# A Nyström attention feeding a squared-ReLU MLP: written step order for the first batch, its inverse folded into A, batch 1's inverse in 32x32 blocks, loads of batches 1 and 2 into an idle buffer

## The chip, the cores and the metric

One core of a Trainium2 chip. The time is the device time of one execution in microseconds, median of several runs. Before the change it is 268.99 us (268.72 to 269.55, three runs). Engines: PE is the matmul engine, DVE VectorE, ACT ScalarE, POOL GpSimd.

## The reference

```python
# q, k, v: (8 batches, 8 heads, 576, 64); m = 32 landmarks of 18 rows each
A  = softmax(q @ k_lm.T / 8)          # 576 x 32
Bm = softmax(q_lm @ k_lm.T / 8)       # 32 x 32
C  = softmax(q_lm @ k.T / 8)          # 32 x 576
Z  = Bm.T / (norm1(Bm) * norminf(Bm) + 1e-6)
for _ in range(6):
    Z = 2 * Z - Z @ Bm @ Z            # Newton inverse
x = (A @ Z @ C @ v)                   # all heads side by side: (4608, 512)
out = square(relu(x @ w_in)) @ w_out  # 512 -> 2048 -> 512
```

## The kernel before

The kernel never forms x. It multiplies the small C v (here cvb) with Z and the input weights to a matrix G, and computes h = G^T A^T straight from it: 16 products "h" of 128 x 576 for a batch (four matmuls of 128x288 each; the timelines count these matmuls), then relu on ACT, square on DVE, and 72 matmuls "out" of the second product. While the MLP of batch b runs, the attention of batch b+1 is prepared in the gaps. A plan of words says in which order PE, DVE and ACT get their instructions:

```python
BATCH0 = (   # h: one product of the MLP; s: its square; a number: so many outs
    "h h s s g h pk s h s h h g s h s h s tk0 h h s pq mk s h s h mq tq0 h s s 2 lm ls s h "
    "tk1 ib tq1 1 h h 1 tt 1 if 2 s 1 sq0 1 jo s 2 sq1 jo s 1 tl jo 2 as0 3 sk1 jl 3 ar0 3 "
    "sk0 2 as1 1 nu at0 2 ar1 nn pk+ 1 cv 1 nu nn1 1 at1 wt pq+ 2 gg0 2 gg1"
)
# pk/pq: cast of the next batch's k/q (with +: of the one after that); tk/tq: its transposes;
# mk/mq: landmark means; ib/if: begin of the inverse; jo: joint step (EY); jl: last joint y;
# nu, nn: Newton steps; tl: tails; as/ar/at: A's row sums, rows, transposes; wt: C's fold; gg: G
```

The words of the inverse and the loads ahead of it, cut:

```python
def products(diagonal, moving):            # eight matmuls 32x32, or two 128x128
    n, w = moving(0).shape[-1], diagonal.shape[-1]
    res = ntile([P, 2, n], place=1, placed=b >= PLACED)
    for qd in range(2):
        for a in range(0, P, w):
            nc.tensor.matmul(res[a:a + w, qd, :], lhsT=diagonal[a:a + w, qd, :], ...)

def stationary(src, tag):                  # batch 0: src itself ("compact")
    ...                                    # other batches: spread on DVE to a block diagonal
with tc.issue_after(one.ins):              # loads after the first piece of w_in
    load_v(0, loaded[0])
    for j in range(1, 4):
        w_in(j)                            # input weights, four pieces
    load_qk(1, loaded[1])
    for j in range(4): ...                 # output weights, four pieces
    load_v(1, loaded[1])
```

The head (batch 0's own attention) is a generator with 17 idle matmuls in it, `warm(n)`, which keep PE's clock up.

The softmax here doesn't subtract the row's maximum and nothing guards it: scores larger than these inputs give would overflow.

Of the kernel before, what the change touches and what calls it, by code (L numbers as in the profile page):

```python
# [17 lines left out]
B = 8  # L18
# [14 lines left out]
PLACED = 1  # L33
BATCH0 = (
    "h h s s g h pk s h s h h g s h s h s tk0 h h s pq mk s h s h mq tq0 h s s 2 lm ls s h "
    "tk1 ib tq1 1 h h 1 tt 1 if 2 s 1 sq0 1 jo s 2 sq1 jo s 1 tl jo 2 as0 3 sk1 jl 3 ar0 3 "
    "sk0 2 as1 1 nu at0 2 ar1 nn pk+ 1 cv 1 nu nn1 1 at1 wt pq+ 2 gg0 2 gg1"
)
BATCH1 = (
    "1 mk 1 h tq0 1 h mq h s tq1 2 lm h s 1 s h ls 1 tt s 1 s h ib sq0 h s 2 h tl 1 if 4 s "  # L40
    "sq1 as0 2 jo h tk0 s 1 h jo 1 s tk1 1 pk+ 1 h jo s pq+ 1 sk0 1 as1 3 sk1 1 jl ar0 s h 1 "
    "h ar1 cv 1 nu h 1 s h nn at0 3 nu 1 s 1 h nn1 3 s 1 wt at1 2 s 2 s 1 gg0 8 gg1 12"
)
EVEN = (
    "2 h h 2 s s 1 mk mq 1 h 1 s 3 lm h ls 1 sq0 h 1 s 1 h 1 s ib 3 s tl h 2 if sq1 h as1 3 "
    "jo sk0 h pk+ 2 s as0 2 s 2 jo s 1 h sk1 h 2 s h pq+ jo cv 2 jl s 1 ar0 2 h h 1 s nu 1 "
    "ar1 2 h nn s 1 s h at0 s 3 nu 3 at1 1 nn1 4 wt s 4 gg0 5 gg1 7"
)
ODD = (
    "2 h s mk 1 h 1 h mq 1 h 2 lm 1 s ls 1 s h s 4 s sq0 1 ib h 1 s tl if 2 h 1 sq1 h pk+ 1 "  # L50
    "jo s as0 s 1 h 1 sk0 2 s 1 h 1 sk1 jo 1 s 1 h as1 h jo s pq+ 1 cv jl 4 h s ar0 1 nu h "
    "ar1 3 s 1 nn h 3 s at0 h 1 nu at1 1 s 1 nn1 3 s 3 wt 4 gg0 8 gg1 15"
)
LAST = (
    "1 h h 1 s 4 h 1 s s h 1 h 2 s 1 h 1 s 6 s 1 h s h 3 h s 2 h 1 s 2 s 1 h 2 s 3 h 2 s h h "
    "1 s 3 h 4 h 7 s s s"
)
PLANS = [BATCH0, BATCH1, EVEN, ODD, EVEN, ODD, EVEN, LAST]
# [3 lines left out]
def kernel(  # L62
# [31 lines left out]
    vts, ects = [], []  # L94
# [7 lines left out]

    def load_qk(b: int, X: dict):

        X["qkt"] = loads.tile([P, H, D], BF16, tag="qkt", name="qkt")

        def tails():
            for src, r0 in ((k, TAIL), (q, 0)):
                nc.gpsimd.dma_start(X["qkt"][r0:r0 + TAIL, :, :],  # L109
                              src[b, :, NC4 * P:S, :].rearrange("h p d -> p h d"))  # L110

        if b > 0:
            tails()
        for nm, src in (("k", k), ("q", q)):
            if b == 0 and nm == "k":
                X[nm + "raw"] = mlp.tile([P, H, NC4, D], F32, tag="gT", name="raw")
            else:
                X[nm + "raw"] = loads.tile([P, H, NC4, D], BF16, tag="raw", name="raw")
            parts = ((0, H // 2), (H // 2, H)) if b == 0 and nm == "q" else ((0, H),)
            for lo, hi in parts:  # L120
                (nc.sync if b == 0 and nm == "k" else nc.gpsimd).dma_start(  # L121
                    X[nm + "raw"][:, lo:hi, :, :],
                    src[b, lo:hi, 0:NC4 * P, :].rearrange("h (p c) d -> p h c d", c=NC4)
                )
            if b == 0 and nm == "k":
                tails()

    def load_v(b: int, X: dict):
        X["vm"] = loads.tile([P, H, NC4, D], BF16, tag="vm", name="vm")
        X["vt"] = vts[b % 2]  # L130
        nc.gpsimd.dma_start(
            X["vm"][:], v[b, :, 0:NC4 * P, :].rearrange("h (p c) d -> p h c d", c=NC4)
        )
        nc.gpsimd.dma_start(
            X["vt"][P - TAIL:P, :, :], v[b, :, NC4 * P:S, :].rearrange("h p d -> p h d")
# [9 lines left out]
    seg = const.tile([P, NC4 + 2, M], BF16, name="seg")  # L145
# [16 lines left out]
    nc.vector.tensor_copy(blk_bf[:], blk[:])  # L162
    ones_bf = const.tile([P, 1], BF16, name="ones_bf")
# [5 lines left out]
    def load_rest(after):  # L169

        def w_in(j):

            r0, f0 = 256 * (j % 2), 1024 * (j // 2)
            return nc.gpsimd.dma_start(
                w_in_bf[64 * (j % 2):64 * (j % 2) + 64, :, f0:f0 + 1024],
                moe_w_in[r0:r0 + 256, f0:f0 + 1024].rearrange("(j d) f -> d j f", d=D),
            )

        with tc.issue_after(masked.ins):
            one = w_in(0)  # L180
# [4 lines left out]
        with tc.issue_after(one.ins):  # L185
            load_v(0, loaded[0])
            for j in range(1, 4):
                w_in(j)
            load_qk(1, loaded[1])
            for j in range(4):  # L190
                nc.gpsimd.dma_start(
                    w_out_bf[:, 4 * j:4 * j + 4, :],
                    moe_w_out[512 * j:512 * j + 512, :].rearrange("(ft fp) c -> fp ft c", fp=P),
                )
            load_v(1, loaded[1])
# [8 lines left out]
    def prepare(b: int, nms=("k", "q"), halves=((0, H),)):  # L204

        X = loaded[b]
        for nm in nms:
            if nm not in X:
                X[nm] = loads.tile([P, NC4, H, D], BF16, tag=nm + "nat", bufs=1, name="nat")
                X[nm + "T"] = attn.tile([P, NC4, NPAIR, P], BF16, tag=nm + "T", name="T")  # L210
            raw = X[nm + "raw"].rearrange("p h c d -> p c h d")
            if b == 0:
                for lo, hi in halves if nm == "q" else ((0, H),):
                    if nm == "q":
                        nc.vector.tensor_copy(X[nm][:, :, lo:hi, :], raw[:, :, lo:hi, :])
                        continue
                    nc.vector.tensor_copy(X[nm][:, 0:2, lo:hi, :], raw[:, 0:2, lo:hi, :])
                    X["cast"] = nc.scalar.copy(X[nm][:, 2:4, lo:hi, :], raw[:, 2:4, lo:hi, :])
                continue
            nc.vector.tensor_copy(X[nm][:], raw)  # L220
            if b >= DMA_T:
                nc.sync.dma_start_transpose(
                    X[nm + "T"].rearrange("p c a t -> p (c a) t"),
                    X[nm].rearrange("p c h d -> p (c h d)"))
        if "k" in nms:
            X["tT"] = attn.tile([P, NPAIR, P], BF16, tag="tT", name="tT")
            if b >= DMA_T:
# [9 lines left out]
    mark, begin, front = [], [], []  # L237

    def in_turn():
        return tc.issue_after(front[0].ins) if front else nullcontext()  # L240

    def attention(b: int, R: dict):
# [4 lines left out]
        first = b == 0  # L247

        def transposed(nm, half):
            if not first:  # L250
                tps = ntile([P, 2, NPAIR, P], BF16, place=int(nm == "q"), placed=b >= PLACED)[:]
            else:
                if half == 0:
                    X["tps"] = psum.tile([P, 4, NPAIR, P], BF16, tag="h", bufs=2, name="tps")
                tps = X["tps"][:, 2 * half:2 * half + 2, :, :]
# [9 lines left out]
        def transposed_tail():  # L265
            tps = ntile([P, NPAIR, P], BF16, placed=b >= PLACED)
# [4 lines left out]
            nc.vector.tensor_copy(X["tT"][:], tps[:])  # L271

        means = ntile([P, 2, NPAIR, M], placed=b >= PLACED)
        STk = small.tile([P, NPAIR, M], BF16, tag="STk", name="STk")

        def segment_means(ti, nm):
# [5 lines left out]
            with in_turn() if b == 1 else nullcontext():  # L282
                for n, (p, c) in enumerate(order):
                    src = X[nm][:, c, 2 * p:2 * p + 2, :] if c < NC4 else X["qkt"][:, 2 * p:2 * p + 2, :]
                    nc.tensor.matmul(  # L285
                        means[:, ti, p, :],
                        lhsT=src.rearrange("p h d -> p (h d)"),
# [566 lines left out]
```

## Time and profile before

| | before |
|---|---|
| span of the profiled run | 267.4 us |
| first h of batch 0 | 24.99 us |
| batch 1's k turned by PE, from | 30.60 us |
| 16th h of batch 0 ends | 38.38 us |
| batch 1's first joint product | 40.02 us |
| first h of batch 1, of batch 2 | 54.81, 84.69 us |

The times come from PE's timeline. From the first h on PE is the bound; what a stage can win is seen from when the next batch's first h starts.

### The profile page before, as it was taken

What the parts mean: (1) busy time and instruction counts of PE and PEld (TensorE: products, weight loads), DVE (VectorE), ACT (ScalarE), POOL (GpSimd) and SP (SyncE); (2) the same over time, 40 slices, a digit from 0 to 9 for tenths busy, and PEclk for the clock granted to TensorE, in tenths of its full rate; (3) what the DMA queues carried; (4) which work ended last, traced back from release to release, by engine and by line L of the source; (5) the groups of instructions that cost most, each with busy time, mean ns of one, the idle gap of its engine ahead of it and who ended that gap; (6) DMA issues with size and microseconds to landing.
All of it is one profiled execution on the core that took longest, in us unless ns stands there. A gap on an engine that the chain in (4) does not pass through costs nothing.

```text
span 267.4 us, 6750 instructions
## 1 busy us (share of the span) xinstructions
PE 247.7 (93%) x2752; PEld 151.0 (56%) x2793; DVE 177.4 (66%) x492; ACT 156.9 (59%) x278; POOL 45.5 (17%) x70
## 2 busy tenths in 40 slices
PE   2988999699989999999999999999999999999994
PEld 0754675276645665466546666466536665555443
DVE  4585989769983699559953798569943887443000
ACT  2366895377844774478345855487535955566210
POOL 8844233402400213021300122000000000000000
PEclk9997999999999999999999999999999999999999
DMA  8999999999699949995996579974421111111222
GB/s 184 177 204 196 204 205 189 206 210 165 103 161 214 126 95 158 142 206 99 201 159 132 78 94 171 168 134 110 90 81 40 42 39 42 39 43 39 78 81 78
DMA packets 69791, 34.65 MB, mean 130 GB/s; under 512 B 37376, under 2 KB 64256, under 8 KB 69760
## 3 DMA queue, kind: packets, MB, share of 16 engines
q0 software_dynamic: 39808, 17.83, 54.9%
q1 hardware_dynamic: 24704, 7.08, 17.7%
q10 hardware_dynamic: 5248, 9.31, 10.5%
q8 instruction: 22, 0.36, 0.6%
q14 instruction: 9, 0.07, 0.1%
HBM read 36.70 MB, written 9.44 MB: 173 GB/s over the span
## 4 chain that ended last, share of the span: by engine, by line
PE 60%; DVE 22%; DMA 6%; ACT 6%; issue 4%; POOL 2%; ACTq 0%; POOLq 0%; DVEq 0%
PE ops L732 18%; PE n L732 15%; PE h L700 14%; DMA raw<-in_q_dram 6%; DVE gT L708 5%; PE g L639 3%; DVE ra L464 3%; ACT r L707 3%; PE n L285 2%; DVE nat L220 2%; PE n L357 2%; PE n L486 2%; DVE ED L348 1%; DVE EY L362 1%; DVE rra L469 1%
## 5 line engine op out<-in xcount | busy, mean ns | idle before, releaser
L707 ACT ACTIVATE r<-h 128x576 bf16<-128x576 f32 x128 | 81.3, 655 | 40.6 <-PE h L700 30.1
L700 PE MATMUL h<-AT,G 128*128 128x288 bf16 x512 | 81.0, 286 | 0.7 <-ACT r L707 0.4
L732 PE MATMUL ops<-w_out_bf,gT 128*128 128x512 bf16 (+1 forms) x301 | 76.7, 368 | 1.0 <-issue 0.5
L708 DVE TENSOR_TENSOR gT<-r 128x576 bf16<-128x576 bf16 x128 | 55.5, 446 | 31.5 <-ACT r L707 30.7
L732 PEld LDWEIGHTS <-gT 128*128 128x128 bf16 x592 | 53.4, 97 | 40.6 <-issue 5.1
L732 PE MATMUL n<-w_out_bf,gT 128*128 128x512 bf16 x253 | 67.6, 379 | 0.9 <-issue 0.5
L700 PEld LDWEIGHTS <-G 128*128 128x128 bf16 x512 | 47.5, 98 | 22.3 <-issue 1.5
L628 DVE CAST G<-g 128x1024 bf16<-128x1024 f32 x14 | 17.1, 1224 | 10.5 <-PE g L639 10.5
L628 ACT CAST G<-g 128x1024 bf16<-128x1024 f32 x14 | 14.2, 1013 | 14.7 <-PE g L639 14.7
L743 ACT COPY o_sb<-ops 128x512 f32<-128x512 f32 (+1 forms) x19 | 10.9, 576 | 12.3 <-PE ops L732 11.9
L743 ACT COPY o_sb<-n 128x512 f32<-128x512 f32 x17 | 10.0, 585 | 10.9 <-PE n L732 10.3
L109 POOL DMA_DIRECT2D qkt<-in_k_dram x8 | 5.7, 708 | 54.3 <-PE n L295 42.7
L440 PEld LDWEIGHTS <-T 128*128 128x128 bf16 x256 | 11.2, 98 | 4.3 <-issue 1.0
L464 DVE TENSOR_REDUCE ra<-EA 128x20 f32<-128x640 f32 (+1 forms) x19 | 13.4, 705 | 0.3
L476 DVE TENSOR_TENSOR an<-EA,rra 128x640 bf16<-128x640 f32 (+2 forms) x17 | 13.1, 771 | 0.0
L440 PE MATMUL n<-bd,T 128*128 128x64 bf16 x256 | 12.7, 193 | 0.2
L357 PEld LDWEIGHTS <-ED 128*128 128x128 bf16 x84 | 7.1, 97 | 9.3 <-DVE ED L348 5.9
L121 POOL DMA_DIRECT2D raw<-in_k_dram x7 | 6.2, 884 | 32.4 <-DVE EY L362 12.4
L444 ACT ACTIVATE EA<-n 128x512 f32<-128x512 f32 x16 | 9.5, 595 | 2.3 <-PE n L440 2.3
L444 ACT ACTIVATE EC<-n 128x512 bf16<-128x512 f32 x16 | 9.6, 598 | 2.1 <-PE n L440 2.1
L220 DVE COPY nat<-raw 128x2048 bf16<-128x2048 bf16 x14 | 10.3, 734 | 0.6 <-DMA raw<-in_q_dram 0.4
L639 PE MATMUL g<-w_in_bf,WT 64*32 64x512 bf16 x232 | 9.6, 390 | 0.7 <-ACT G L628 0.4
(121 smaller groups left out, 268.1 us busy)
## 6 DMA issues: line engine op xcount, KB each, us to landing
out_dram<-o_sb ACTq DMA_DIRECT2D x31, 256.0 KB, 3.2
vm<-in_v_dram POOLq DMA_DIRECT2D x8, 512.0 KB, 16.4
raw<-in_k_dram POOLq DMA_DIRECT2D x7, 512.0 KB, 9.9
raw<-in_q_dram POOLq DMA_DIRECT2D x7, 512.0 KB, 13.8
w_in_bf<-in_moe_w_in_dram POOLq DMA_DIRECT2D x4, 512.0 KB, 10.7
w_out_bf<-in_moe_w_out_dram POOLq DMA_DIRECT2D x4, 512.0 KB, 16.1
out_dram<-o_sb ACTq DMA_DIRECT2D x9, 128.0 KB, 3.2
raw<-in_k_dram SPq DMA_DIRECT2D x1, 1024.0 KB, 5.3
```

The lines of the kernel that those rows point to most:

```text
L220: nc.vector.tensor_copy(X[nm][:], raw)
L440: nc.tensor.matmul(sc[:, c, j, :, :], lhsT=X[nm + "T"][:, c, p, :], rhs=BD[:, 1 if nm == "q" else 0, p, 0:64], start=True, stop=True)
L444: nc.scalar.activation((EA if nm == "q" else EC)[:, qd, 0:NC4, :], sc.rearrange("p c j i m -> p c (j i m)"), AF.Exp, scale=SCALE)
L464: nc.vector.reduce_sum(ra[:, quads, lo:hi, :], EA[:, quads, lo:hi, :].rearrange("p q c (h m) -> p q c h m", m=M), axis=AX.X)
L476: nc.vector.tensor_tensor(an[:, i, lo:hi, :].rearrange("p c (h m) -> p c h m", m=M), EA[:, i, lo:hi, :].rearrange("p c (h m) -> p c h m", ...
L628: last = (act, dve)[n % 2](G[:, :, n * 512:n * 512 + 512], gg[:])
L639: nc.tensor.matmul(g[i][M * p:M * p + M, :], lhsT=WT[64 * i:64 * i + 64, i, M * p:M * p + M], rhs=w_in_bf[64 * i:64 * i + 64, p, n * 512:n ...
L700: last = nc.tensor.matmul(h[:, j, 0:HALF], lhsT=G[:, qd, f * P:(f + 1) * P], rhs=AT[:, qd, j * HALF:(j + 1) * HALF], start=(qd == 0), stop ...
L707: nc.scalar.activation(r.rearrange("p (j t) -> p j t", j=2), h[:, :, 0:HALF], AF.Relu)
L708: return lambda: nc.vector.tensor_tensor(gT[:, f, o:o + S], r[:], r[:], ALU.mult)
L732: nc.tensor.matmul(ops, lhsT=gT[:, f, t * P:t * P + P], rhs=w_out_bf[:, f, i * n:i * n + n], start=(f == 0), stop=(f == NF - 1))
L743: nc.scalar.copy(o_h, ops)
```

## The change

The intent: (1) the head's steps become a written list without idle matmuls, whose chain ends in V^T A^T (a product az on A), so that G can be made before the inverse is done; (2) batch 1 uses the compact 32x32 form of batch 0; (3) k and q of batches 1 and 2 are loaded into an idle buffer, and batch 2's casts move from stage 0 to stage 1; (4) the input weights come in eight pieces, in a written order; (5) new written orders for all later stages.

```diff
+COMPACT = 1                       # batches 0 and 1 compact
+HEAD = ("ck tk0 ek0d mk cq0 tt tk1 ek1d cq1 et mq tq0 eq0d lm sk0 tq1 ls ib ... jl cr cbd nu "
+        "row:1:0:3 ct at:0 row:1:3:5 ea0d fv at:1 g:0 ea1d gl0d gf1a gf0d az gl1a")
+LOADS = "w00 v0 w02 w10 w01 w11 q1 w12 w03 w13 o0 o1 o2 o3 v1"
 BATCH0 = (
-    "h h s s g h pk s h s h h g s h s h s tk0 ... 1 sq0 1 jo s 2 sq1 jo s 1 tl jo 2 as0 3 sk1 jl 3 ar0 3 "
-    "sk0 2 as1 1 nu at0 2 ar1 nn pk+ 1 cv 1 nu nn1 1 at1 wt pq+ 2 gg0 2 gg1"
+    "h h pk s h g:1 h s s h h s h s g:2 h s s tk0 h h pq g:3 s s mk h h mq s tq0 h 1 lm s s "
+    "1 h tk1 s tq1 2 ls h ib 2 s tt h if sq0 1 jo s 1 sq1 1 s jo 2 jo tl as0 2 jl 1 sk0 4 "
+    "sk1 1 nu 1 ar0 at0 as1 1 nn ar1 cv nu nn1 3 wt 1 at1 gg0 5 gg1 5"
 )
@@ head: G from C, the inverse on A
+            elif name == "g":
+                if n[0]:
+                    gg = psum.tile([P, 2, 512], F32, tag="h", bufs=2, name="g")
+                else:
+                    gg = [ntile([P, 512], placed=b > 0)[:] for e in range(2)]
+                g_of(st["CT"], gg, n[0], 0)
+            elif name == "az": ...   # 16 matmuls 32x32x288: v times A^T, four copies to AZ
@@ end of the loads
+            for i in range(2):
+                ct = const.tile([P, 2, NC4 + 1, P], BF16, name="ct%d" % i)
+                nc.gpsimd.memset(ct[:], 0.0)
```

(Cut: helpers, the later plans, and variants switched off by `DMA_A = DMA_C = 9`; `ct` belongs to one of those and is not read.)

## The prediction

> **What bounds the kernel now.** I read the page first, then the busy time by stretch, then the timelines of TensorE and VectorE around the thin stretch, last the chain of waits. Columns of a stretch: its bounds, its length, then busy time (and count) of PE, PEld, DVE, ACT, POOL, then clock, DMA share, GB/s.
>
> ```profile
> span 267.4 us, 6750 instructions
> PE 247.7 (93%) x2752; PEld 151.0 (56%) x2793; DVE 177.4 (66%) x492; ACT 156.9 (59%) x278; POOL 45.5 (17%) x70
> GB/s 184 177 204 196 204 205 189 206 210 165 103 161 214 126 95 158 142 206 99 201 159 132 78 94 171 168 134 110 90 81 40 42 39 42 39 43 39 78 81 78
> ...
> 24.99:54.81 29.82, 26.13 (x360) 16.89 (x358) 25.58 (x67) 20.52 (x37) 11.41 (x15) 0.99 1.45 200
> 54.81:84.69 29.88, 28.77 (x332) 17.98 (x336) 23.43 (x63) 20.06 (x34) 4.69 (x6) 1.00 1.20 164
> ```
>
> TensorE is the bound from about 25 us on. The first matmul of the first MLP product (h) starts at 24.99 us; batch 1's first h at 54.81, batch 2's at 84.69, then 113.09, 143.50, 171.90, 202.03, 229.82, and the last evacuation ends near 264. So there are three parts: a head of 25 us, whose length is a dependency chain; a first stage of 29.8 us; and seven stages in which PE is busy 204.3 of 208.5 us (from 55.0 to 263.5), where at most some 4 us could be had.
>
> The first stage is the weak one. Its own matmuls are few. The plan gives it 64 h matmuls and 35 of the second product (out). At full clock an h takes 0.123 us (8 in about 0.98), an out 0.216 (16 in 3.45 near the end). The table splits stages into these two and the rest, transposes on PE taken apart (36 of 56 ns, 2.0 us, for batches 1 and 2, made in the first two stages):
>
> | stage | length | h | out | transposes, late G | left for the next batch's attention, and idle |
> |---|---|---|---|---|---|
> | batch 0 | 29.8 | 7.8 | 35: 7.6 | 2.7 | 11.7 |
> | batch 1 | 29.9 | 7.8 | 64: 13.8 | 2.0 | 6.3 |
> | batch 2 | 28.4 | 7.8 | 68: 14.7 | 0 | 5.9 |
> | batch 3 | 30.4 | 7.8 | 76: 16.4 | 0 | 6.2 |
>
> Batch 0 thus spends about 5.5 us more than its kind. The timeline of PE and that of DVE say where:
>
> ```profile
> 47.88 0.22 PE L357 MATMUL n<-v,BT 128*128 128x32 bf16 x2 [0.24 <-DVE v L406]
> 49.77 0.21 PE L357 MATMUL n<-y,ED 128*128 128x32 bf16 x2 [1.67 <-DVE ED L348]
> ...
> 48.09 0.90 DVE L220 COPY nat<-raw 128x2048 bf16<-128x2048 bf16 x1 [0.26 <-DMA raw<-in_k_dram]
> 48.91 0.15 DVE L522 RECIPROCAL rc<-n 128x2 f32<-128x2 f32 x1
> 49.09 0.29 DVE L528 TENSOR_TENSOR cvb<-n,rc 128x128 bf16<-128x128 f32 x1
> 49.30 0.41 DVE L348 TENSOR_TENSOR ED<-n,blk_bf 128x256 bf16<-128x256 f32 x1
> ...
> 51.75 0.69 DVE L220 COPY nat<-raw 128x2048 bf16<-128x2048 bf16 x1 [0.37 <-DMA raw<-in_q_dram]
> 52.36 1.22 DVE L628 CAST G<-g 128x1024 bf16<-128x1024 f32 x1
> ```
>
> The reader sees batch 1's inverse, a chain PE, DVE, PE, and inside it the cast of batch 2's k, which waited for its load; PE stands 1.67 us behind it. The cast of batch 2's q does the same to the G copy. The chain of waits holds the same thing as one piece:
>
> ```profile
> 36.69 15.03 DMA raw<-in_q_dram
> ```
>
> The 15 us look like a gain for an earlier issue. They are not, see the rival below.
>
> **What the Trainium skill says.**
> 1. "DMA: Bandwidth & Descriptors", section "Issuing engines are not separate DMA queues": all DMAs interleave on the same 16 engines. The same page, "Where 436 GB/s comes from", gives about 358 GB/s as HBM's share per core. The trace agrees: all that precedes batch 2's q (q and k of three batches, v of two, both weights) is 17.8 MB of fp32 read, and it had landed at 51.75 us; from about 2 us that is 359 GB/s. (The page's GB/s counts the bf16 written, so 200 there is near 360 to 400 read.) Up to 55 us DMA is full.
> 2. "TensorE: Matmul & The Clock Gate", "Part 1: The HAM clock gate": half rate until about 3.4 us of sustained work. The trace agrees: the three idle matmuls of 512 columns at 9.53 us took 1.49 us, about 0.43 apart, against 0.216 later; at 24.99 eight h took 1.26 us up to the next group, not 0.98; the clock of 20 to 30 us is 0.83.
> 3. "VectorE: DVE Perf Modes", "Rules for kernel authors": in chains of DVE operations, minimize their count. Here each small one costs 0.17 to 0.29 us.
>
> **The change, part by part.**
>
> *Head.* The order of PE, DVE and ACT is now written. All 17 warming matmuls go. The sixth Newton step, the spread of Z (zt), C's fold (wt), WT and the G that hung on them leave the chain; G is made from normalized C early. In their place, the chain ends in V's last step (fv), 16 matmuls of 32x32x288 with A^T, and four copies of 128x288. From the end of the last y, before: zt 0.3, wt 0.4, WT 0.4, idle matmuls 0.7, g 0.6, G copy and AT 1.1: h starts 3.3 us after y was done at 21.66. After: az first half 0.5 to 0.6, copy 0.4, so about 1.3 us after v, if G and AT are there.
> But DVE fills the chain: from EY on it has five joint or v steps (1.4 us), y and v (0.5), sums (2.0), four row products (1.7), reciprocals (0.7), cvb (0.3), two AT copies (0.9), G pieces (0.6): 8.1 us. EY should be complete near 14.7 us instead of 15.46, because the add of 1e-6 is gone (it rides on a matmul) and the copy of q's transposes stands before the softmax. 14.7 + 8.1 + waits of about 0.7 + az with its first copies, so far as they lie behind DVE's last G piece, 0.6 gives a first h at 24.1: **0.9 us** earlier. Without warming, the clock is low there for perhaps 2.4 us of h work instead of 1.1: 0.4 us back. Net **0.5 us**.
>
> *First stage.* Batch 1 turns compact: BT, four ED and two ED from nu vanish from DVE (5 x 0.29 + 2 x 0.38 = 2.2 us), also cs, rows and c (0.6); two copies U on ACT (0.4) come. The casts of batch 2 (0.9 + 0.69) move to the start of the next stage. DVE, 25.6 busy of 29.8, is relieved of 4.4 us, mostly inside the chain. Walking it from the end of the 16 h (38.3 before, 37.8 after): three joint steps at 0.7 instead of 0.95 us each, no ED after nu, no cast in the second Newton step (1.0, and 0.26 wait). Before, EY 39.2, last joint y 43.9, first Newton y 47.5, last y 50.2, g 51.4. After: 38.3, 41.9, 45.0, 46.7, and with the three outs ahead of wt g at 47.9. Ten outs (2.2 us) stand among the g instead of four, so batch 1's h starts 3.1 to 3.3 us after g: near 51.0 instead of 54.8, **3.8 us** earlier, of which 0.5 is the head's.
>
> *Second stage.* It gets two casts more (1.4 us on DVE, 23.4 of 29.9 busy): perhaps 0.3 us lost. *Later stages.* Same matmuls in another order: between 0 and 1 us of the 4 idle, I take 0.6. Copies for later batches and the tail are unchanged in kind.
>
> Sum: 0.5 + 3.3 - 0.3 + 0.6 = 4.1 us: 269.0 - 4.1 = **264.9 us**.
>
> **Rivals.**
> *Early loads win the 15 us.* For: the piece in the chain. Against: the read rate is at its ceiling throughout, and the same bytes lie ahead of q of batch 2 in the new order. Landing moves by the dips of the GB/s row (177, 189) only, 1 us at most. If it were wrong, batch 1 could start at 49 and the time be 262.
>
> *DMA takes the place of the wait removed.* If the chain gets faster than I say, the next wait is v of batch 1, which lands after 15.5 MB, near 45 us, and which c_values needs at 45.0; and q of batch 2 at 51.7, needed by its cast at 51 to 52. Both limits are close: a shorter first stage gains nothing past some 5 us in all. The slices of the input weights (w_in in 8 pieces) land in time: the last after 10.6 MB, 31 us, needed for the fourth G at about 31. A late one would stop PE for 1 us; the time would be 266 to 267.
>
> *The head gains nothing or loses.* DVE's 8.1 us is as long as before (7.3 and less), and the clock is cold throughout; if DVE slips 1 us, only the first stage's gain stays: 266.
>
> *The written orders of the later stages are better than I can see.* For: seven stages leave 4 us idle, some of it at the end of each inverse. Then 263.
>
> **Range and chances.** The first stage's 3.3 has an uncertainty of some 1.5 (bounded above by 5.5 and the loads), the head's 0.5 one of 0.8, the later stages one of 0.7: together about 1.8 us, so 80% lies within 2.4: 262.5 to 267.2. More than 2% faster means below 263.6, a gain of 5.4 against 4.1: about one in four. Slower would need the orders to be broken somewhere; one in fifty.
>
> **What the profile after would show.** Right: first h near 24.1 us and low clock around it; batch 1's first h near 51.0; stage 0's remainder falling from 11.7 to about 8.5; no cast of batch 2 inside batch 1's inverse; batch 2's q still landing at 50 to 52 us, GB/s still near 200 up to 55 us; stages 2 to 7 within 0.3 us of before each. Wrong: a first h after 25, PE waiting for v or for w_in in the first stage, batch 1's mean matmuls of batch 2 held by its casts, or later stages shorter by more than 1 us in all.

## The result, and the profile after

The changed kernel is correct. Median 270.79 us (270.00 to 271.21, 4 runs) against 269.04 (4 runs); the ratio is 1.006, 95% interval 1.0031 to 1.0089. A ratio is the mean time of one kernel's fast runs over that of the other's in the same rounds, so it is not quite the ratio of the medians quoted. Later, e17 has two slow runs, e18 one, and the kernel before one in the fifth call; medians and ranges below leave them out, as the ratios do.

The page after: first two lines of part 1, the clock row (tenths of full speed in 40 slices) and the GB/s row.

```profile
span 269.5 us, 6893 instructions
PE 252.9 (94%) x2843; PEld 153.1 (57%) x2843; DVE 176.2 (65%) x487; ACT 157.4 (58%) x276; POOL 50.5 (19%) x77
PEclk9985899889999999999999999999999999999999
GB/s 185 140 198 193 205 207 191 213 190 76 61 200 119 206 76 165 170 193 71 177 157 197 91 81 178 104 211 175 118 80 41 39 41 39 41 40 39 80 78 78
```

The clock row of before has one 7, where the one after has a 5 and four 8s:

```profile
PEclk9997999999999999999999999999999999999999
```

Busy time by stretch, after (bounds, length, PE, PEld, DVE, ACT, POOL, clock, DMA share, GB/s):

```profile
10.00:15.00 5.00, 3.90 (x56) 3.67 (x53) 3.32 (x11) 1.51 (x4) 4.13 (x7) 1.00 1.22 148
...
20.00:25.00 5.00, 4.18 (x63) 2.41 (x61) 4.22 (x14) 2.03 (x6) 3.25 (x5) 0.50 1.58 190
...
50.00:55.00 5.00, 4.05 (x50) 1.60 (x48) 2.97 (x10) 1.69 (x3) 0.00 (x0) 0.74 1.57 213
...
24.60:57.93 33.33, 31.30 (x405) 17.78 (x405) 22.66 (x56) 21.22 (x38) 12.95 (x16) 0.89 1.43 201
```

PE is "busy" for 4.18 of the 5 us before the first h, yet its clock is at half. The first stage (last line) answers to the 29.82 of before, with PE busy 31.30 instead of 26.13 and DVE 22.66 instead of 25.58. PE's and DVE's timelines show where:

```profile
24.60 3.04 PE L814 MATMUL h<-AZ,G 128*128 128x288 bf16 x12 [0.56 <-DVE AZ L787]
...
53.42 1.05 PE L797 MATMUL g<-w_in_bf,WT 64*32 64x512 bf16 x16
54.41 1.95 PE L843 MATMUL n<-w_out_bf,gT 128*128 128x512 bf16 x5
56.28 0.63 PE L797 MATMUL g<-w_in_bf,WT 64*32 64x512 bf16 x16
...
57.93 1.14 PE L814 MATMUL h<-AT,G 128*128 128x288 bf16 x8
```

Twelve h matmuls, three products h, took 3.04 us, 0.25 each, where 0.123 is the full rate; the first 16 G matmuls at 53.42 took 1.05 us and the next 16, at 56.28, 0.63. PE ran at half rate twice: around the first h, and at the end of batch 1's inverse.

```profile
25.81 0.69 DVE L275 COPY nat<-stage 128x2048 bf16<-128x2048 bf16 x1 [0.90 <-DMA stage<-in_k_dram]
...
45.72 0.82 DVE L565 TENSOR_REDUCE ra<-EA 128x20 f32<-128x640 f32 x1 [0.43 <-ACT EA L553]
46.57 0.28 DVE L570 RECIPROCAL rra<-ra 128x20 f32<-128x20 f32 x1
46.77 0.16 DVE L412 SCALAR_TENSOR_TENSOR y<-EY,n 128x64 bf16<-128x64 bf16 x1
```

Batch 1's k now makes its cast wait 0.90 us. The last joint y (done at 46.93) comes 5 us later than my 41.9, right behind A's row sums. The casts of batch 2 have left the inverse and wait for nothing at 58.12, as intended. The load of batch 1's k was issued later, as POOL's timeline shows, first before, then after:

```profile
13.69 0.89 POOL L121 DMA_DIRECT2D raw<-in_k_dram x1 [0.77 <-DMA w_in_bf<-in_moe_w_in_dram]
```

```profile
17.21 0.89 POOL L127 DMA_DIRECT2D stage<-in_k_dram x1 [3.03 <-DMA vm<-in_v_dram]
```

The later stages did well: from batch 1's first h to the end, 211.6 us (269.5 - 57.9) against 212.6.

I measure every kernel below by four points of PE's timeline: first h; the first transposes of batch 1's k ("turn"); the first joint product on EY; batch 1's first h. "Start" is first h to turn, "middle" turn to EY product, "inverse" EY product to batch 1's h.

| kernel | first h | start | middle | inverse | batch 1's first h |
|---|---|---|---|---|---|
| before | 24.99 | 5.61 | 9.42 | 14.79 | 54.81 |
| after | 24.60 | 7.74 | 10.53 | 15.06 | 57.93 |
| e1 | 23.54 | 7.89 | 10.66 | 13.60 | 55.69 |
| e2 | 25.42 | 7.25 | 9.58 | 13.95 | 56.20 |
| e3 | 24.84 | 7.20 | 10.53 | 13.87 | 56.44 |
| e4 | 25.19 | 7.30 | 10.92 | 16.72 | 60.13 |
| e6 | 24.46 | 7.70 | 10.36 | 13.61 | 56.13 |
| e7 | 23.29 | 7.14 | 10.60 | 15.03 | 56.06 |
| e8 | 23.30 | 7.30 | 10.53 | 13.61 | 54.74 |
| e9 | 23.55 | 7.45 | 12.00 | 13.01 | 56.01 |
| e10 | 23.54 | 7.39 | 11.99 | 13.29 | 56.21 |
| e11 | 23.59 | 7.75 | 10.55 | 13.87 | 55.76 |
| e12 | 23.30 | 7.01 | 10.37 | 14.07 | 54.75 |
| e13 | 23.59 | 7.26 | 10.61 | 14.32 | 55.78 |
| e14 | 23.59 | 7.38 | 10.45 | 14.82 | 56.24 |
| e15 | 24.12 | 6.19 | 12.33 | 14.07 | 56.71 |
| e16 | 23.51 | 5.88 | 11.99 | 14.82 | 56.20 |
| e17 | 23.06 | 8.67 | 11.83 | 15.30 | 58.86 |
| e18 | 23.53 | 7.46 | 10.39 | 14.07 | 55.45 |
| e19 | 23.54 | 8.59 | 11.82 | 14.34 | 58.29 |

Each row is one profiled execution. The same warmed head gave a first h between 23.06 and 24.12 in fourteen of them, so differences under half a microsecond in one row mean little. In the change and in the ten variants of it that I compared, the stages from batch 1's first h on have the same lengths within 0.05 us, but for the second one of e9 and e10 (0.16 more, by their later casts): what follows is decided in the head and the first stage.

### The profile page after: what moved, and what is told of

Its sections match the earlier page's. It is cut to its first block, busy times and chain, and to the rows that moved or that the text cites.

```text
span 269.5 us, 6893 instructions
## 1 busy us (share of the span) xinstructions
PE 252.9 (94%) x2843; PEld 153.1 (57%) x2843; DVE 176.2 (65%) x487; ACT 157.4 (58%) x276; POOL 50.5 (19%) x77
## 4 chain that ended last, share of the span: by engine, by line
PE 84%; DVE 9%; DMA 2%; ACT 2%; issue 1%; DVEq 0%
PE ops L843 24%; PE h L814 22%; PE n L843 21%; PE g L797 3%; PE n L335 2%; PE n L523 2%; DMA stage<-in_k_dram 2%; PE n L589 2%; DVE ra L565 2%; PE n L407 2%; PE tps L309 1%; DVE an L577 1%; DVE gT L819 1%; PE n L309 1%; ACT r L818 1%
## 5 line engine op out<-in xcount | busy, mean ns | idle before, releaser
L843 PE MATMUL ops<-w_out_bf,gT 128*128 128x512 bf16 (+1 forms) x320 | 83.5, 368 | 0.0
L843 PEld LDWEIGHTS <-gT 128*128 128x128 bf16 x592 | 54.0, 98 | 41.6 <-issue 6.3
L843 PE MATMUL n<-w_out_bf,gT 128*128 128x512 bf16 x272 | 73.9, 383 | 0.0
L814 PE MATMUL h<-AT,G 128*128 128x288 bf16 x448 | 70.7, 286 | 0.0
L696 ACT CAST G<-g 128x1024 bf16<-128x1024 f32 x14 | 14.2, 1014 | 13.1 <-PE g L797 13.1
L127 POOL DMA_DIRECT2D raw<-in_k_dram x5 | 4.5, 890 | 53.5 <-DVE ED L398 27.9
L565 DVE TENSOR_REDUCE ra<-EA 128x20 f32<-128x640 f32 (+3 forms) x19 | 13.2, 701 | 0.7 <-ACT EA L553 0.4
L814 PE MATMUL h<-AZ,G 128*128 128x288 bf16 x64 | 11.3, 316 | 1.1 <-DVE AZ L787 0.6
L309 PEld LDWEIGHTS <-nat 128*128 128x128 bf16 x96 | 7.3, 112 | 8.3 <-DVE nat L710 7.5
L309 PE MATMUL tps<-ident_bf,nat 128*128 128x128 bf16 x32 | 4.1, 309 | 7.7 <-DVE nat L710 7.5
```

The costliest lines, as they stand in the source:

```text
L127: d = queue.dma_start(dst, src)
L309: nc.tensor.transpose(tps[:, i, p, :], X[nm][:, 2 * half + i, 2 * p:2 * p + 2, :].rearrange("p h d -> p (h d)"), ident_bf[:],)
L565: nc.vector.reduce_sum(ra[:, quads, lo:hi, :], EA[:, quads, lo:hi, :].rearrange("p q c (h m) -> p q c h m", m=M), axis=AX.X)
L696: (act, dve)[n % 2](G[:, :, n * 512:n * 512 + 512], gg[:])
L814: nc.tensor.matmul(h[:, j, 0:HALF], lhsT=G[:, qd, f * P:(f + 1) * P], rhs=AT[:, qd, a0 + j * HALF:a0 + (j + 1) * HALF], start=(qd == 0), s ...
L843: nc.tensor.matmul(ops, lhsT=gT[:, f, t * P:t * P + P], rhs=w_out_bf[:, f, i * n:i * n + n], start=(f == 0), stop=(f == NF - 1))
```

## The experiments

Eighteen kernels ran, in six calls; the kernel before ran in the same rounds of each. All are correct. Medians are of six runs, but for e17 (four fast ones) and e18 (five). Each call ran on a chip of its own, so medians of different calls compare loosely; the ratios to before are of the same rounds.

### First call: the clock, the compact form

**e1**: the change with idle matmuls (`w:n`, about 20) back in the head.

```diff
-    "ck tk0 ... sk0 tq1 ls ib eq1a if sq0 jo sq1 sum:0:0:2 ..."
+    "w:4 ck tk0 ... sk0 w:1 tq1 ls w:1 ib eq1a if sq0 w:1 jo sq1 w:1 sum:0:0:2 ... az w:2 gl1a"
```

> The changed kernel with warming matmuls (128x512, on zeros) put back into its head, 4 ahead of the k cast and some 20 in the gaps of the chain; nothing else differs. Theory (clock): the changed kernel's trace has the granted clock at 0.50 from 20 to 25 us and 0.65 from 25 to 30, and 12 h matmuls took 3.04 us where they need 1.5; warm, the clock should be above 0.9 from 20 to 30, the 16th h of batch 0 should end about 2 us earlier than at 42.2, batch 1's first h come near 56 instead of 57.9, and the time fall by 1.5 to 2.5 us to 268.5 or so. Rival (the written order itself is slow: the first stage is held by ScalarE and by the order): the clock rises but the time moves by less than 0.5 us. Second rival (the fillers stand in the chain's way): first h later than 24.6 by as much as is won.

268.92 us (268.19 to 269.31), ratio to before 0.9982 [0.9950, 1.0014]: 1.9 us less than the change by medians. Its h run at full rate, and the first h comes 1.06 us earlier:

```profile
23.54 1.22 PE L814 MATMUL h<-AZ,G 128*128 128x288 bf16 x8
...
28.16 1.14 PE L814 MATMUL h<-AZ,G 128*128 128x288 bf16 x8 [1.12 <-DVE G L637]
```

But "start" is no shorter (7.89 against 7.74): PE stands 1.12 us for DVE's copy of G, which stands behind the cast of k, which waited 2.46 us for its load. What the clock gave, the load partly took: at the EY product e1 is only 0.78 us ahead (42.09 against 42.87). The rest of the lead at batch 1's first h is the second dip, 1.4 us, which this profile lacks (inverse 13.60 against 15.06) though e1 changes nothing there. So the 1.9 us are not the idle matmuls' alone; see e6 and e7.

**e2**: the kernel before with `warm` doing nothing.

```diff
-        for _ in range(n):
+        for _ in range(0):
             nc.tensor.matmul(idle[:, 0:width], ...)
```

> The kernel before with its 17 warming matmuls taken out and nothing else changed. Theory (clock): the clock is low through the head and up to some 28 or 29 us instead of 26; the h matmuls of the first 4 us take 0.25 us each; batch 1's first h comes 1 to 2.5 us later than 54.81 and the time is 270 to 271.5. Rival (order): the time stays within 0.5 us of 269.0.

270.35 us (269.77 to 272.17), ratio 1.0046 [1.0011, 1.0081]. Eight h matmuls take 2.10 us:

```profile
25.42 2.10 PE L700 MATMUL h<-AT,G 128*128 128x288 bf16 x8
```

So the 17 idle matmuls were worth 1.2 us to the kernel before (0.3 to 2.2 by the interval); the change threw them out. The clock column of this profile reads 1.00 throughout: the durations decide, not the column.

**e3**: the change with seven idle matmuls at the end of batch 1's inverse (I wrote eight; the words add up to seven, and the trace has seven).

```diff
-    "sk1 1 nu 1 ar0 at0 as1 1 nn ar1 cv nu nn1 3 wt 1 at1 gg0 5 gg1 5"
+    "sk1 1 nu 1 ar0 at0 as1 1 nn w:1 ar1 cv w:2 nu w:2 nn1 3 w:1 wt 1 at1 w:1 gg0 5 gg1 5"
```

> The changed kernel with 8 filler matmuls of 128x512 put between the steps at the end of batch 1's inverse (after nn, cv, nu, nn1, wt, at1 in BATCH0) and the head as it is. Theory (clock): the second dip (0.74 from 50 to 55 us, 0.91 from 55 to 60; 16 g took 1.05 instead of 0.63, 5 outs 1.95 instead of 1.24) goes away, which is worth about 2 us less some 0.8 of filler that does not fit into gaps: 1 us faster than the changed kernel. Rival: the dip is where PE would wait for VectorE anyway (y, zt, WT, G), so the clock rises and batch 1's first h stays at 57.9 or gets later; time unchanged or 0.5 us slower.

269.77 us (268.82 to 270.46), ratio 1.0013 [0.9981, 1.0045]: 1.0 us less than the change by medians. The same G now runs at full rate:

```profile
53.03 0.62 PE L798 MATMUL g<-w_in_bf,WT 64*32 64x512 bf16 x16
```

The second dip is real, and filling it seems to pay in the change as it stands (the two intervals against before overlap).

**e4**: the change with `COMPACT = 0`.

> The changed kernel with batch 1's inverse in the old form (blocks spread to 128x128, COMPACT = 0), as before. If the compact form is worth what I reckoned (2.2 to 2.8 us of VectorE inside batch 1's chain), this is 1.5 to 2.5 us slower than the changed kernel. If 32x32 matmuls count little for the clock, then the second dip (50 to 57 us) vanishes here and the kernel is as fast or up to 1 us faster. If VectorE was not what held the chain, it is equal.

274.43 us (273.05 to 275.10), ratio 1.0182 [1.0148, 1.0217]. By the ratios the compact form is worth 1.2%, 3.3 us, a little more than the 2.8 us of DVE work I had counted (2.2 and 0.6). In the profiles e4 starts batch 1 only 2.2 us later (60.13 against 57.93), 0.6 of it from the head, which the edit leaves alone. The second dip is there too:

```profile
55.93 1.05 PE L797 MATMUL g<-w_in_bf,WT 64*32 64x512 bf16 x16
```

So it needs neither 32x32 products in batch 1 nor the faster chain. The compact form is not free on PE: a product of eight 32x32 matmuls occupies it for 0.15 to 0.17 us (from 42.87 to the next group at 43.04) where two of 128x128 took 0.07 (40.95 to 41.02 in before), and the fp32 norm matmuls add 0.50 (40.38 to 40.88). My sum had nothing for these.

### Second call: where G is accumulated, when k is cast

**e6**: without warming, the later G products in the small PSUM banks instead of h's two. **e7**: the same with the warmed head of e1. **e8**: e7 with the cast of k behind G n=1.

```diff
 e6:
-                if n[0]:
-                    gg = psum.tile([P, 2, 512], F32, tag="h", bufs=2, name="g")
-                    gg = [gg[:, e, :] for e in range(2)]
-                else:
-                    gg = [ntile([P, 512], placed=b > 0)[:] for e in range(2)]
+                gg = [ntile([P, 512], placed=b > 0)[:] for e in range(2)]
 e8 also:
-    "h h pk s h g:1 h s s h h s h s g:2 ..."
+    "h h s h g:1 h s pk s h h s h s g:2 ..."
```

> The changed kernel with the last three G products of batch 0 put back from the double buffer of h into two of the small PSUM banks, as before; no warming. In the warmed run the 16 h of batch 0 still take 17.8 us (23.54 to 41.3) where the kernel before needs 13.4, and PE waits at each of these products for r or for the G copy. Theory (G takes a place of h, so each of the three stops the alternation of h and r): the three waits go, batch 0's 16th h ends 1 to 2 us earlier than 42.2, the time falls by 0.8 to 2 us to 269 to 270. Rival (the clock hides it): while the clock is low PE is the bound there, so less than 0.5 us. Second rival (the waits are ScalarE's own work, whatever the bank): nothing.

> Warming in the head (as e1, which gave 268.9) and the G products in the small banks. Theory: the two gains add up, because with a full clock PE no longer hides the waits: 1 to 2 us below e1, near 267.3; 16th h of batch 0 at 39.5 instead of 41.3. Rival (the cast of batch 1's k, which waited 2.46 us for its load in e1 ahead of G and gT on VectorE, is the bound): less than 0.5 us better than e1, with the wait still there.

> As e7, and the cast of batch 1's k moved behind the second G product, to where its load has landed. Theory of the load: in e1 k landed at 26.4, VectorE stood 2.46 us and PE 1.12 us behind it; this goes, worth another 0.5 to 1.2 us: 266 to 267, which would beat the kernel before by 2 us and more. Rival (k's later steps are then what is late): same time as e7.

e6 269.32 us (268.15 to 269.96), ratio 0.9990 [0.9967, 1.0013]; e7 269.98 (269.36 to 271.58), 1.0036 [1.0008, 1.0064]; e8 269.24 (268.01 to 270.27), 0.9989 [0.9964, 1.0015]. By medians e6 gains 1.5 us on the change, though on another chip, but its profile shows only 0.35 us up to the EY product, 0.14 of it in the head; the rest is the missing second dip. So the banks themselves are not shown to matter. e6 and e7 differ by the idle matmuls alone: the first h comes 1.17 us earlier (23.29 against 24.46), yet the median is 0.7 us longer. e7 had the dip in its profile (inverse 15.03), e6 and e8 had not (13.61 both), although all do the same there: the dip comes in some executions and not in others and is worth 1.4 us. The runs' mean granted clock goes with it: 0.994 in five of e7's six runs and in three of e8's, which took 269.33 to 270.27 where those at 1.000 took 268.01 to 269.15. So warming the head is not shown, by itself, to shorten this kernel's time: what it gains, the dip can take back. e7 and e8 missed the 267.3 and 266 to 267 I expected.

### Third call: the order of before

**e9**: e8 with BATCH0 from mk on in the order of before (without batch 2's casts, with fewer outs late in the inverse). **e10**: e9 with three idle matmuls late in the inverse.

```diff
-    "... pq g:3 s s mk h h mq s tq0 h 1 lm s s 1 h tk1 s tq1 2 ls h ib 2 s tt h if sq0 ..."
+    "... pq g:3 s mk s h s h mq tq0 h s s 2 lm ls s h tk1 ib tq1 1 h h 1 tt 1 if 2 s 1 sq0 ..."
```

> As e8 (warmed head, G in the small banks, k's cast later), and batch 0's plan from the mean matmuls on put back into the order of the kernel before (softmax of batch 1 ahead of the squares, four fewer outs ahead of the 16th h), with the casts of batch 2 left where the change put them, in the next stage. In e8 batch 1's first EY stood complete at 41.1 us although h began at 23.3; before it was at 39.2 with h at 25.0. Theory (the new order starts batch 1's inverse late, and the compact chain then only wins that back): EY at 38 to 38.5, batch 1's first h at 52 to 53 instead of 54.7, the time 1.5 to 2.5 us below e8 in the same rounds, near 267. Rival (PE is full there: the compact form's 32x32 products and the fp32 matmuls for the norm cost PE 1.4 us more, so the order only moves waits about): less than 0.7 us better than e8.

> As e9 with three fillers of 128x512 in the thin end of batch 1's inverse (after cv, nu and nn1). In e7 the clock was 0.66 from 50 to 55 us and batch 1's first h came at 56.06, in e8, which is the same up to there, it was full and h came at 54.74: a dip costs 1.3 us and comes in some executions only. Theory: the fillers keep the clock up in every execution, so the spread shrinks and the mean is 0.3 to 0.8 us below e9. Rival: they cost their 0.65 us and the mean is 0.3 us above e9.

e9 269.46 us (269.29 to 269.59), ratio 0.9993 [0.9967, 1.0018]; e10 269.64 (269.05 to 270.26), 1.0000 [0.9970, 1.0030]. "Middle" grew from 10.53 to 12.00. The compact form's norm matmuls want a bank that ACT still empties, and tT's copy then waits for PE:

```profile
38.76 0.43 PE L422 MATMUL n<-tiny,blk 128*128 128x64 f32 x2 [1.13 <-ACT T L655]
```

```profile
41.54 0.42 DVE L657 COPY tT<-n 128x512 bf16<-128x512 bf16 x1 [1.65 <-PE n L319]
```

The old order does not fit the compact form: that the new order alone starts the inverse late, as I had thought, is refuted. e10's fillers gained nothing; e9 shows no dip to fill (granted clock 0.997 or more in all its runs).

### Fourth call: outs behind the 16th h, fillers

**e11**: e8 with e3's fillers. **e12**: e8 with four of the six outs ahead of the 16th h moved behind it. **e13**: both.

```diff
-    "... mq s tq0 h 1 lm s s 1 h tk1 s tq1 2 ls h ib 2 s tt h if sq0 1 jo s 1 sq1 1 s jo 2 jo tl as0 ..."
+    "... mq s tq0 h lm s s h tk1 s tq1 1 ls h ib 1 s tt h if sq0 2 jo s 2 sq1 2 s jo 3 jo tl as0 ..."
```

> The earlier variant with warmed head, G products in the small banks and the cast of batch 2's k moved behind G n=1, plus the eight filling matmuls at the end of batch 1's inverse. Clock theory: the dip at 50 to 57 us, which came in some executions and not in others, never comes: batch 1's first h at 54.6 to 54.8 us in the profile, no h, g or out at half rate near 52 to 56, time 268.3, ratio to before 0.995 to 0.998. Rival, that the fillers cost as much as they save because PE is the bound there (8 x 0.22 us): 269.3 to 269.8.

> The same variant without fillers, but of the six second-product matmul groups that stand ahead of the 16th h four are moved behind it, between the joint steps. If those groups are what delays the 16th h and with it EY (my reading of the order), the 16th h ends at 39.3 to 39.7 instead of 40.4, EY comes 0.5 to 0.9 earlier than 40.7 to 41.1, and batch 1 starts near 54.0: 268.4 without a dip. Rival, that DVE's chain (squares, softmax, landmarks) sets EY whatever PE does: the 16th h comes earlier, EY stays within 0.2 us, time as without the move, 269.2.

> Both of the two edits before. If clock and order are both real costs of the first stage: batch 1's first h at 53.8 to 54.2, time 267.5 to 268.0, ratio near 0.994. If only the fillers work: as the first of these. If neither works: 269.2 to 269.8.

e11 268.91 us (268.08 to 269.17), ratio 0.9983 [0.9959, 1.0008]; e12 268.98 (268.05 to 271.26), 1.0011 [0.9974, 1.0048]; e13 269.04 (268.65 to 269.35), 0.9989 [0.9966, 1.0013]. In e12 the 16th h ended at 39.82 instead of 40.50, EY stood 0.67 us earlier (40.04 against 40.71) and its first product came 0.45 earlier, but the last joint y did not move at all. DVE's line is the same in e8 and e12:

```profile
43.98 0.82 DVE L565 TENSOR_REDUCE ra<-EA 128x20 f32<-128x640 f32 x1 [0.43 <-ACT EA L553]
```

The rival, that EY would stay within 0.2 us, was wrong. The moved outs ate the gain: seven of them, not four, now stand between the first and the third joint product, and the third starts at 42.97 in both. The tail's product follows it, then ACT's exponentials, then these row sums, then y. The fillers narrowed the spread (e11 1.1 us, e13 0.7, e8 2.3, e12 3.2), no run of e11 and e13 had a granted clock below 0.997, and the median stayed within 0.4 us.

### Fifth call: order of the inverse, order of the start

All three on e12. **e14**: the tail's product one joint step earlier, A's first row sums behind the last joint y, the second ones behind wt. **e15**: G n=1 behind the first h and n=2 behind the sixth, and both pieces of w_in for n=2 ahead of batch 1's q and k (in e12 one of them was behind). **e16**: both.

```diff
 e14:
-    "... s jo 3 jo tl as0 2 jl 1 sk0 4 sk1 1 nu 1 ar0 at0 as1 1 nn ar1 cv nu nn1 3 wt 1 at1 gg0 5 gg1 5"
+    "... s jo tl 3 jo 1 sk0 2 jl as0 1 nu sk1 2 nn ar0 cv 1 nu at0 1 nn1 2 wt as1 1 ar1 gg0 3 at1 4 gg1 6"
 e15:
-LOADS = "w00 v0 w02 w10 w01 w11 q1 w12 w03 w13 ..."
+LOADS = "w00 v0 w10 w01 w11 w02 w12 q1 w03 w13 ..."
-    "h h s h g:1 h s pk s h h s h s g:2 h s s tk0 ..."
+    "h g:1 h s h s h s pk h s h g:2 s h s h s tk0 ..."
```

> The variant with the outs moved behind the 16th h, and in batch 1's inverse only: the tail's product one joint step earlier, the first row sums of A behind the last joint y, the second ones behind the product with C. If VectorE's order held the chain: last joint y at 44.1 to 44.3 instead of 45.03, first Newton y near 45.8 instead of 48.47, last y near 47.5 instead of 49.94, batch 1's first h at 52 to 53 instead of 54.75; the time gains less, as outs that filled gaps must then be done elsewhere: 267.0 to 268.0, ratio 0.992 to 0.995. Rival, that TensorE's own work is the bound there (it was busy some 18 of the 20 us before batch 1's start): the y come earlier but batch 1's first h moves by less than 0.8 us and the time by less than 0.8: 268.3 or more.

> The same base, and at the start of the MLP only: the second product of G stands after the first h instead of the third, the third G after the sixth h, and the two pieces of the input weights for it are loaded ahead of batch 1's k and q. If the late G and the late weights hold PE there: no wait on G's copy near 26.7 nor on w_in near 29.3, the eighth h ends about 0.8 us earlier than in the base (near 30.0), the 16th h and EY 0.5 us earlier, but with the inverse's order unchanged the y stay where they are: batch 1's first h within 0.3 of 54.75, time within 0.4 of 269. Rival: the later k (by some 3 us) stops the cast and the transposes near 28 to 31, then EY comes 0.5 to 1 us later and the time is 269.5 to 270.

> Both edits. If both orders cost time and TensorE has room: batch 1's first h at 51.5 to 52.5, time 266.5 to 267.5, ratio near 0.990. If PE's own work is the bound: 268 or more.

e14 269.56 us (268.95 to 272.24), ratio 1.0022 [0.9974, 1.0069]; e15 270.09 (268.75 to 271.27), 1.0018 [0.9974, 1.0062]; e16 269.73 (268.89 to 271.86), 1.0024 [0.9975, 1.0073]. e14's first Newton y came at 47.27 instead of 48.47, its last y at 49.82 instead of 49.94: what was won is lost behind A's first transposes, and A's second row, now ahead of the last G, makes PE wait 0.52 us. In this run, moving A's work on DVE only moved who waits. e15 shortened the start from 7.0 to 6.2 us, e16 to 5.9: the late G, with the load order that was changed along with it, costs 0.8 to 1.1 us there. Then PE stood for the pieces of w_in that now load behind q and k (e15):

```profile
32.48 0.37 PE L793 MATMUL n<-w_in_bf,CT 64*32 64x512 bf16 x1 [0.41 <-DMA w_in_bf<-in_moe_w_in_dram]
33.79 0.41 PE L793 MATMUL n<-w_in_bf,CT 64*32 64x512 bf16 x7 [0.94 <-DMA w_in_bf<-in_moe_w_in_dram]
```

### Sixth call: all weights first

**e17**: e12 with G n=1 behind the first h, n=2 behind the fifth (not the fourth, as I wrote below), and all of w_in ahead of batch 1's q and k; the cast of k also moved, from behind the fourth h to behind the seventh. **e18**: e17 with the tail's product a joint step earlier. **e19**: e18 with e3's fillers.

```diff
-LOADS = "w00 v0 w02 w10 w01 w11 q1 w12 w03 w13 ..."
+LOADS = "w00 v0 w10 w01 w11 w02 w12 w03 w13 q1 ..."
 e18 also:
-    "... 2 s jo 3 jo tl as0 2 jl ..."
+    "... 2 s jo tl 3 jo as0 2 jl ..."
```

> Same base as the last call (warmed head, small banks, outs behind the 16th h), with the second G after the first h, the third after the fourth h, and all pieces of the input weights ahead of batch 1's q and k. If the load order held the start: no PE wait on w_in, eighth h done 6.0 us after the first (near 29.5), k's cast near 28 as in the kernel before, 16th h near 39.3, batch 1's first h at 54.2 to 54.8 as the inverse's own waits stay: 268.5. Rival, that the read rate is the limit whatever goes first: batch 1's k, now behind 1.5 MB more, stops PE at the transposes by 1 us or more near 30, and the time is 269.5 to 270.5.

> The run before with the tail's product one joint step earlier. If its exponentials hold the row sums and so the last joint y: that y comes 0.6 to 1.0 us earlier, batch 1's first h 0.5 to 1.0 earlier, 267.7 to 268.2. Rival: PE's outs ahead of the joint steps decide, the y stays within 0.2.

> The run before with the eight fillers at the end of the inverse. If random low clock spreads the single runs: highest minus lowest of six runs under 1.2 us, against 2 to 3.3 us without fillers in the last two calls; the median within 0.5 us of the run before, as the fillers cost what they save on average.

e17 269.66 us (269.02 to 272.08; two slow runs, 273.11 and 273.96, left out), ratio 1.0021 [0.9978, 1.0064]; e18 270.61 (268.71 to 272.58; one slow run, 273.95, left out), 1.0089 [1.0043, 1.0136]; e19 269.68 (268.73 to 271.61), 1.0014 [0.9981, 1.0047]. No wait for w_in is left, but k is late; e17 first, then e18:

```profile
31.73 0.88 PE L309 MATMUL n<-ident_bf,nat 128*128 128x128 bf16 x8 [2.39 <-DVE nat L275]
32.40 2.13 PE L810 MATMUL h<-AZ,G 128*128 128x288 bf16 x8
```

```profile
30.99 0.62 PE L309 MATMUL n<-ident_bf,nat 128*128 128x128 bf16 x8 [1.18 <-DVE nat L275]
31.45 1.14 PE L810 MATMUL h<-AZ,G 128*128 128x288 bf16 x8
```

After a wait of 2.39 us the next eight h matmuls take 2.13 us (e19: 2.31, then 2.13), after one of 1.18 they take 1.14: in these three executions half rate followed the longer wait. Not all of the wait is the load's. DVE's cast waited 0.89 us for DMA in e17 (0.30 in e18, 0.81 in e19) and then took 2.02 us instead of 0.69, beside the change's new memset of `ct` on POOL (28.82 to 31.12 us):

```profile
28.82 2.30 POOL L256 MEMSET ct<- 128x1280 bf16 x2
```

```profile
29.64 2.02 DVE L275 COPY nat<-stage 128x2048 bf16<-128x2048 bf16 x1 [0.89 <-DMA stage<-in_k_dram]
```

The other traces settle what the memset does. In twelve variants (e1, e4, e6 to e11, e13, e14, e17, e19) a cast of k or q began while it ran; each ended 0.54 to 0.56 us after the memset did, and so took 0.99 to 2.02 us. In the change, e3 and e15, where none overlapped it, casts took 0.68 to 0.69. So about 1.3 of e17's 2.02 us are the memset's, and "the read rate is the limit whatever goes first" is shown for 0.3 to 0.9 us only. No run without the memset was made; in the change itself it met no cast. e18's tail changes nothing (EY product to batch 1's h 14.07 us, as in e12). The runs spread with the granted clock: the three fast runs of e17 and e18 at 0.987 took 272.08 to 272.58 us, the four at 1.000 268.71 to 269.91. e19 spread over 2.9 us even with fillers, more than the 1.2 I expected: they guard the inverse, not the wait for k.

No version clearly beats the kernel before: the best, e1 and e11, have ratios of 0.998 with intervals that reach 1.

## Why the prediction was wrong, point by point

Predicted 264.9 us, range 262.5 to 267.2, with one chance in fifty for "slower"; measured 270.79, slower by 0.6%. The steps that it named, as intervals (EY by the start of its instruction on DVE, each y by its end):

| step | predicted | after | e8 |
|---|---|---|---|
| first h at | 24.1 | 24.6 | 23.3 |
| to the end of the 16 h | 13.7 | 17.6 | 17.2 |
| to EY | 0.5 | 0.2 | 0.2 |
| to the last joint y | 3.6 | 4.5 | 4.5 |
| to the first Newton y | 3.1 | 3.4 | 3.4 |
| to the last y | 1.7 | 1.5 | 1.5 |
| to g | 1.2 | 1.5 | 1.2 |
| to batch 1's first h | 3.1 | 4.5 | 3.4 |

The differences after minus predicted add up to 6.9 us at batch 1's first h (57.93 against 51.0). The later stages then returned 1.0 instead of my net 0.3 (0.6 less 0.3): 264.9 + 6.9 - 0.7 = 271.1, and the profiled run took 271.21.

**The head** (0.5). The direction was right: the first h came 0.4 us earlier. But that near hit is partly luck, two misses that cancel: EY was complete at 16.14 us and not at 14.7 (before 15.46), and from there to the first h it took 8.5 us and not 9.4. The clock term was mis-sized. I gave "2.4 us of h work instead of 1.1: 0.4 us back" for the missing idle matmuls. They cost 1.06 us before the first h already (e1; 1.17 in e7 against e6), because the chain's own matmuls run slow too: the 16 of az took 1.15 us in the change and 0.67 in e1. My estimate took only the h.

**The first stage** (3.3). This step failed, and mostly at its first term: "38.3 before, 37.8 after" for the end of the 16 h, which simply carried the 13.3 us of before over (13.7 with the clock's 0.4). It became 17.6. In before two quarters of G are multiplied ahead of the first h, the third after the second h and the fourth after the sixth, and all input weights load ahead of batch 1's k. In the change the second comes after the third h, the third after the seventh and the fourth after the tenth, and the last weights load behind q and k. Before first, the last three quarters of G and the end of the h:

```profile
24.43 0.63 PE L639 MATMUL n<-w_in_bf,WT 64*32 64x512 bf16 x8
26.25 0.41 PE L639 MATMUL n<-w_in_bf,WT 64*32 64x512 bf16 x8
29.27 0.41 PE L639 MATMUL n<-w_in_bf,WT 64*32 64x512 bf16 x8
37.24 1.14 PE L700 MATMUL h<-AT,G 128*128 128x288 bf16 x8
```

```profile
27.57 0.63 PE L797 MATMUL g<-w_in_bf,CT 64*32 64x512 bf16 x8
31.22 0.41 PE L797 MATMUL g<-w_in_bf,CT 64*32 64x512 bf16 x8
34.18 0.41 PE L797 MATMUL g<-w_in_bf,CT 64*32 64x512 bf16 x8 [0.25 <-ACT r L818]
41.58 0.65 PE L814 MATMUL h<-AZ,G 128*128 128x288 bf16 x4
```

I wrote that "G is made from normalized C early", which holds only for n=0. e15 and e16 show 0.8 to 1.1 us for it, with the load order changed too. Of the 2.1 us by which "start" grew, the cold clock alone can take 1.6 (e2 against before: 7.25 and 5.61), but with warming and the change's own start the start stays at 7.0 to 7.9, held then by k, G and w_in: these causes overlap and can't be added. "Middle" grew by 1.1 us; in it lie the fourth quarter of G (0.35) and the fp32 norm matmuls (0.5) that my sum left out. Six outs of 0.2 us each instead of three stand ahead of the 16th h. So what failed is known; how the 3.9 us divide among these causes stays open.

**The inverse itself.** From the end of the 16th h to batch 1's first h I walked 13.2 us instead of 16.4; it took 15.7 in the change and 14.2 in e8, without the dip. From the EY product it took 13.6 us without the dip, 15.0 with it, against 14.8 before. The relief of DVE is real (e4), but its busy time in the stage fell by 2.9 us and not by the 4.4 I counted. And part of the 14.8 was waiting for batch 2's loads: e2, the old form in the old order but 2 us later, took 13.95 with casts that waited for no load. The joint steps at "0.7 instead of 0.95" came out at 1.13, 0.70 and 0.93 (products at 42.87, 44.00, 44.70, 45.63): outs and scores stand between them on PE, and A's row sums stand ahead of the last y on DVE. The second dip took 1.4 us. What brings it is not shown: e4, with the slower chain, has it too.

**The rivals.** "Early loads win the 15 us" was rightly refused: no gain came from there, and GB/s stayed near 200 up to 60 us. "DMA takes the place of the wait removed" was nearly right, but earlier in the stage than I looked: not v of batch 1 or q of batch 2, which nobody waited for, but batch 1's k (0.90 us in the change, 2.46 in e1) and, with a faster start, the last pieces of w_in. "The head gains nothing or loses" was right about the cold clock.

**Later stages** (0.6 - 0.3). Better than I said, 1.0 us in sum. My "stages 2 to 7 within 0.3 us of before each" was wrong for four of the six, most for two neighbours (28.88 against 30.13, 29.46 against 27.79), between which the new plans move outs. One sum of mine was off as well: up to the last piece of w_in 10.1 MB are read, not 10.6.

**Still open.** Why batch 1's k is issued 3.5 us later: in the trace its issue waits for an earlier load, and GB/s at 10 to 15 us is 148 against 188 before. Eight smaller weight loads instead of four stand ahead of it, but no run tested that. What brings the second dip. And how much e17's order would give without the memset.

## What to carry to other kernels

When a change shortens a latency chain on the matmul engine, count what it takes away from the clock: idle matmuls that look like waste were worth 1.2 us to the kernel before, and in the change they brought the first h 1.1 us earlier, though not surely the end. Keep fills of unread buffers out of the busy stretches: a memset on POOL held a cast on DVE until it was done. Do not carry an interval over from the old plan to the new one because its matmuls are the same; walk its first products again, look how far ahead of its use each operand is made and loaded, and price the small matmuls that replace vector work. Test a dip that comes in some executions by the spread of many runs, not by one profile.

## What the Trainium skill lacked or had wrong

- "TensorE: Matmul & The Clock Gate", "Part 1: The HAM clock gate", speaks of busy and idle windows of about 3.4 us. Here PE was busy by the profile for 4.18 of 5 us (20 to 25 us) at a clock of 0.50, much of it in 32x32 products, transposes and one-column matmuls. "Part 4: PE-mode transpose" of the same page says that transposes do not count as busy in the same way, which agrees in kind; that other small matmuls may not keep the clock either is not said. The runs do not separate the kinds.
- Same page: an idle time of 2.39 us, with 0.9 us of transposes after it, was followed by h matmuls at half rate (8 in 2.13 us), one of 1.18 us was not (1.14). With the transposes not counted the first is 3.1 us from h to h (29.34 to 32.40), near the page's window.
- No page sets the two forms of the inverse side by side: eight 32x32 products occupy PE 0.15 to 0.17 us where two 128x128 ones take 0.07.
- The granted clock in the records can read 1.00 while an h matmul takes 0.26 us (e2). The same page warns that these trace events are unreliable; this is a number for it.
- "GPSIMD Engine Reference", "2. Architecture", says that GpSimd's SBUF ports are shared with VectorE. The runs agree and give a size: in twelve of them a 128x2048 bf16 copy on VectorE that began during the memsets ended 0.54 to 0.56 us after them (2.02 us instead of 0.69 in e17, whose memsets took 2.30). In e12 it was the other way round: the copy took 0.77 and the memsets 2.80.
